# An attention read feeding a squared-ReLU expert: the hidden chunk leaves PSUM once, and the written order is replaced

## The chip, the core and the metric

The kernel runs on one NeuronCore of a Trainium2 chip. TensorE (PE in the rows, its weight loads PEld), VectorE (DVE), ScalarE (ACT), GpSimd (POOL) and SyncE (SP, which issues the DMAs) work side by side and wait for one another on semaphores. The metric is the time of one execution on the device, in microseconds (us).

## The reference, cut to what is computed

```python
# x: (8, 8, 512, 64), state: (8, 8, 32, 64); w_in (512, 2048), w_out (2048, 512) are 8-byte floats
scores = x @ state.T / 8;  a = softmax(scores);   xread = a @ state     # per batch and head
scores2 = state @ x.T / 8; a2 = softmax(scores2); sread = a2 @ x
out = concatenate([xread, sread], axis=2)          # (8, 8, 544, 64)
X = out.transpose(0, 2, 1, 3).reshape(8 * 544, 512)
h = maximum(X @ w_in, 0)
return (h * h) @ w_out                             # (4352, 512)
```

## The kernel before, in words

The tokens are worked in nine blocks: blocks 0 to 7 are the 512 tokens of one batch, block 8 holds the 256 state tokens of all batches. The 2048 hidden columns are cut into 16 chunks of 128. Precision is kept by pairs: a number is held as a high part (type fp32r) and a low part, the rest, and a product is three products, high by high, high by low and low by high.

- `hidden(blk, fc)` makes one chunk of X @ w_in, 128 hidden columns by 512 tokens, in one PSUM bank `ph`: 6 products in blocks 0 to 7 (the weights there are state times w_in, and the softmax values `k_hi`, `k_lo` are the moving side), 8 in block 8. Then it makes the squared ReLU as a pair `g_hi`, `g_lo`. Before the change there are two ways. A chunk in the list `square` has three ScalarE passes, ReLU and square inside PSUM and a cast to `g_hi`; any other has a ReLU to SBUF (`r`), VectorE's product of the ReLU and `r` inside PSUM, and ScalarE's square of `r` as `g_hi`. In both, VectorE takes `g_hi` from the bank for `g_lo`, and only then is the bank free. One chunk (0.1) makes its low part by a product with minus the identity instead (`minus_hi`, list `g_pe`).
- `accumulate(blk, fc)` multiplies the pair by the chunk of w_out, 12 products of 512 columns into four banks `acc` (6 in block 8). In blocks 0 and 1 it comes in two parts, `g_hi` first.
- There are two banks for `ph` (`ps_h`, shared with the dummy products, `later_w2` and part of the joined rows), three buffers for `g_hi` and `g_lo`, and two for the tag `g`, which holds `r` and block 8's `cross`.
- Weights arrive as 8-byte floats and are decoded: a clamp, a ScalarE pass, two integer instructions of VectorE (`decode_wi` for w_in, with a store of the result to `win_f`; `prep_wo` for w_out).
- `warm(i)` is a step of two transposes of the identity whose result nobody reads; there are 12 such steps.
- The order on every engine, SP's DMAs too, is written out: `PLAN` lists steps, and each name runs that step up to its next `yield`. Since `LOOSE_FROM` is never met, every instruction is kept in that order. `SECOND` lists for which keys an operation goes to its second engine (`pick(key, first, second)`), the clamps, low parts, evacuations and softmax steps among them.

An instruction that waits therefore holds all that stands behind it on its engine. All instructions have the line L429 in the profile, that of the helper which issues them, so they are told apart by their tiles.

Of the kernel before, what the change touches and what calls it, by code (L numbers as in the profile page):

```python
# [25 lines left out]
    ident start.0 start.0 load_raw.0 decode_wi.0 load_states.0 load.0.1 decode_wi.0 prep.0.0 load_raw.1  # L26
        warm.0 neg_ident load.0.1 decode_wi.0 load_states.0 warm.5 warm.2 prep.0.1 load_states.0 prep.0.0
        load_wo.1 decode_wi.0 prep.0.0 prep.0.1 decode_wi.0 warm.11 load_wo.0 warm.6 decode_wi.1 prep.0.0
        decode_wi.1 decode_wi.1 warm.8 start.1 prep.0.1 states.0 prep.0.1 load_raw.2 prep_wo.1 states.0
        scores.0 decode_wi.1 start.1 load.1.1 prep_wo.1 prep_wo.1 decode_wi.1 prep_wo.0 direct_w2.0  # L30
        keep_s.0.0 keep_s.0.1 decode_wi.2 transposed_scores.0.1 direct_w2.0 direct_w2.0 warm.10
        transposed_scores.0.0 direct_w2.0 direct_w2.0 prep_wo.1 prep_wo.1 direct_w2.0 load.1.1 load_raw.3
        load_wo.3 direct_w2.0 second_w2.0 softmax.0.1 second_w2.0 softmax.0.1 warm.4 softmax.0.1 second_w2.0
# [4 lines left out]
        warm.3 load_wo.4 decode_wi.3 prep_wo.0 softmax.0.0 prep_wo.1 decode_wi.3 scores.1 keep_s.1.0
        keep_s.1.1 softmax.0.1 decode_wi.3
    hidden.0.0 decode_wi.3 hidden.0.0 hidden.0.0 transposed_scores.1.0 hidden.0.0 load_raw.5 load_wo.6  # L40
        prep_wo.2 prep_wo.2 softmax.1.0 hidden.0.0 prep_wo.0 transposed_scores.1.1 softmax.1.1 softmax.1.1
        decode_wi.3 load_wo.8
    hidden.0.1 softmax.1.0 hidden.0.1 hidden.0.0 accumulate.0.0 softmax.1.1 prep_wo.2 decode_wi.4 hidden.0.1
        hidden.0.1 direct_w2.1 softmax.1.1 direct_w2.1 decode_wi.4 direct_w2.1 prep_wo.3 direct_w2.1
        direct_w2.1 decode_wi.4 direct_w2.1 direct_w2.1 hidden.0.1 prep_wo.2 hidden.0.1 softmax.1.0
        second_w2.1 accumulate.0.0 exp_s.0.1
    hidden.0.2 prep_wo.2 second_w2.1 second_w2.1 hidden.0.2 softmax.1.0 softmax.1.1
    hidden.0.3 prep_wo.3 prep_wo.5 softmax.1.1 hidden.0.2 softmax.1.0 decode_wi.4 accumulate.0.1
        accumulate.0.1 softmax.1.1 decode_wi.4 softmax.1.1 hidden.0.2 hidden.0.3 softmax.1.0 hidden.0.2
        prep_wo.2 second_w2.1 decode_wi.5 second_w2.1 hidden.0.3 exp_s.0.1 load_raw.6 prep_wo.3 second_w2.1  # L50
        prep_wo.3 hidden.0.2 accumulate.0.2 prep_wo.4 softmax.1.0 prep_wo.3 softmax.1.0 decode_wi.6
        decode_wi.5 accumulate.0.2 hidden.0.3 prep_wo.5 prep_wo.4 prep_wo.3
# [6 lines left out]
    hidden.1.2 direct_w2.2 direct_w2.2 decode_wi.10 prep_wo.5 hidden.1.1 hidden.1.2 load_wo.7 accumulate.1.0
        hidden.1.1 accumulate.1.1 load_raw.7 decode_wi.6 hidden.1.2  # L60
    hidden.0.4 exp_s.0.0 hidden.1.2 decode_wi.10 decode_wi.7 decode_wi.7 prep_wo.6 hidden.1.2 second_w2.2
        hidden.1.2 prep_wo.4 decode_wi.7 hidden.0.4 prep_wo.5 exp_s.0.0 second_w2.2 load_raw.11 second_w2.2
        second_w2.2 decode_wi.7 transposes.0 load_states.2 decode_wi.7 accumulate.1.1 second_w2.2 prep_wo.8
        decode_wi.11 hidden.0.4 hidden.0.4 hidden.0.4 prep_wo.4 second_w2.2 prep_wo.6
# [14 lines left out]
    hidden.1.5
    hidden.1.4 prep_wo.10 states.2 hidden.1.5 prep_wo.12 hidden.1.4 hidden.1.4 accumulate.0.6 direct_w2.4  # L80
        decode_wi.12 hidden.1.4 transposes.0 prep_wo.9 decode_wi.12 decode_wi.14 prep_wo.10 hidden.1.4
        hidden.1.5 prep_wo.10 direct_w2.5 hidden.1.4 accumulate.0.6 load_raw.13 accumulate.0.7 hidden.1.5
        hidden.1.5 decode_wi.14 hidden.1.5 prep_wo.12 exp_s.1.1 prep_wo.9 accumulate.0.7 load_w2.0.4
        accumulate.0.7 accumulate.0.7 prep_wo.10 prep_wo.12
    hidden.1.6 load_w2.0.4 accumulate.0.7 prep_wo.10 decode_wi.12 accumulate.0.7
    hidden.1.7 hidden.1.7 hidden.1.6 accumulate.0.7 accumulate.0.7 hidden.1.6 accumulate.0.7 load_n.0.0
        load_n.0.1 decode_wi.14 prep_wo.12 prep_wo.13 prep_wo.12 hidden.1.6 decode_wi.14 hidden.1.6
        decode_wi.13 decode_wi.13 load_w2.0.4 hidden.1.7 accumulate.0.7 accumulate.1.4 prep_wo.11 prep_wo.12
        hidden.1.7 prep_wo.11 accumulate.1.4 load_raw.15 prep_wo.13 accumulate.1.5 exp_s.1.1 decode_wi.14
        hidden.1.6 hidden.1.7 load_w2.0.5 hidden.1.7 accumulate.1.5 decode_wi.13 decode_wi.13 prep_wo.13  # L90
        prep_wo.11 decode_wi.13 prep_wo.11 accumulate.1.6 direct.6+read.0 exp_s.1.0 sread.0 direct_w2.6
        accumulate.1.6 prep_wo.11 accumulate.1.7 accumulate.1.7 direct_w2.6 decode_wi.15 decode_wi.15
        sread.0 load_wo.14 direct_w2.6 decode_wi.15 sread.0 accumulate.1.7 direct_w2.6 load_w2.0.5
    hidden.0.8 prep_wo.13 hidden.0.8 hidden.0.8 accumulate.1.7 load_wf.1.1 decode_wi.15 hidden.0.8
        accumulate.1.7
    hidden.0.9 accumulate.1.7 decode_wi.15 hidden.0.9 direct.7 accumulate.1.7 prep_wo.11 hidden.0.8
        split_states load_w2.0.6 accumulate.1.7 hidden.0.9 sread.0 load_w2.0.5 load_w2.1.6 accumulate.1.7
        exp_s.1.0 hidden.0.8 accumulate.0.8
# [1291 lines left out]
```

## Time and profile before

| | us |
|---|---|
| median of 3 runs (lowest, highest) | 649.44 (648.93, 649.57) |
| the profiled execution, its own time | 649.0 |
| its span, first to last instruction | 647.2 |
| TensorE busy in the span | 634.5 |
| VectorE, ScalarE, GpSimd busy | 365.7, 348.0, 125.9 |

The span is 1.8 us shorter than the profiled execution's time. Busy times overlap one another; a time of an engine counts for the total only where another engine waits for it.

### The profile page before, as it was taken

The page shows a single profiled execution, that of the slowest core. Times are in us where ns is not written, and L with a number is a line of the kernel's source. Part 1 is how long each engine was busy: PE and PEld are TensorE (multiplying, and loading weights), DVE is VectorE, ACT ScalarE, POOL GpSimd, SP SyncE. Part 2 cuts the span into 40 slices and gives each one's busy share as a digit, 9 for nine tenths or more (in the row PEclk, how much of TensorE's full clock was granted, in tenths as well). Part 3 has the DMA queues.
Part 4 walks back from the last instruction along what each step waited for, and adds up shares of the span by engine and source line. Part 5 has one row for each costly group of instructions (what it writes and reads, how often), then busy time and mean ns, then how long its engine had stood idle before and what let it go on. Part 6 is the DMA issues. An engine that isn't in the chain of part 4 may idle for free.

```text
span 647.2 us, 10790 instructions
## 1 busy us (share of the span) xinstructions
PE 634.5 (98%) x4004; PEld 511.6 (79%) x4004; DVE 365.7 (56%) x658; ACT 348.0 (54%) x678; POOL 125.9 (19%) x96
## 2 busy tenths in 40 slices
PE   5899999999999999999999999999999999999997
PEld 4677777888788878778878878788777888888886
DVE  3999896775756467475347545456354554442322
ACT  3888867656655455365444544455444355444433
POOL 1584343413310220022001310021010101001000
PEclk9999999999999999999999999999999999999999
DMA  8877898988866684463665635352779814240103
GB/s 270 314 233 243 291 283 290 265 266 252 228 179 182 196 253 110 99 169 100 147 163 146 149 82 158 86 124 73 239 239 271 216 46 115 67 145 34 32 1 97
DMA packets 151859, 110.87 MB, mean 171 GB/s; under 512 B 93056, under 2 KB 126080, under 8 KB 151808
## 3 DMA queue, kind: packets, MB, share of 16 engines
q1 hardware_dynamic: 151568, 109.93, 58.7%
q8 instruction: 31, 0.51, 0.3%
q10 hardware_dynamic: 240, 0.26, 0.1%
q14 instruction: 20, 0.16, 0.1%
HBM read 71.89 MB, written 38.27 MB: 170 GB/s over the span
## 4 chain that ended last, share of the span: by engine, by line
PE 95%; DVE 3%; DMA 1%; issue 0%; SPq 0%; ACT 0%; DVEq 0%
PE acc L429 58%; PE ph L429 30%; PE w2ps L429 2%; PE w4ps L429 2%; PE pr L429 1%; PE st L429 1%; DMA xn<-in_x_dram 1%; DVE wf L429 1%; DVE s L429 1%; DVE sp L429 1%; DVE m L429 0%; PE px L429 0%; DVE dec L429 0%; SPq L429 0%; PE pw L429 0%
## 5 line engine op out<-in xcount | busy, mean ns | idle before, releaser
L429 PE MATMUL acc<-wo,g_hi 128*128 128x512 f32 x1090 | 322.4, 391 | 0.0
L429 PEld LDWEIGHTS acc<-wo,g_hi 128*128 128x128 f32 x1090 | 202.8, 188 | 47.4 <-issue 3.4
L429 PE MATMUL acc<-wo,g_lo 128*128 128x512 f32 x545 | 196.7, 389 | 0.0
L429 PE MATMUL ph<-k_hi,w 128*128 128x512 f32 x512 | 172.8, 390 | 0.2 <-DVE w L429 0.2
L429 DVE TENSOR_TENSOR g_lo<-ph,g_hi 128x512 fp32r<-128x512 f32 (+1 forms) x143 | 92.9, 655 | 83.4 <-ACT g_hi L429 81.2
L429 PEld LDWEIGHTS acc<-wo,g_lo 128*128 128x128 f32 x545 | 102.1, 188 | 21.9 <-issue 0.4
L429 ACT ACTIVATE ph<-ph 128x512 f32<-128x512 f32 (+1 forms) x150 | 83.1, 554 | 59.3 <-PE ph L429 49.7
L429 PEld LDWEIGHTS ph<-k_hi,w 128*128 128x128 f32 x512 | 96.0, 188 | 21.4 <-DVE w L429 0.6
L429 PE MATMUL ph<-k_lo,w 128*128 128x512 f32 x256 | 99.8, 390 | 0.0
L429 DVE SCALAR_TENSOR_TENSOR ph<-ph,r 128x512 f32<-128x512 f32 (+1 forms) x69 | 46.7, 676 | 87.8 <-ACT r L429 87.8
L429 ACT ACTIVATE r<-ph 128x512 f32<-128x512 f32 (+1 forms) x69 | 40.3, 583 | 86.6 <-PE ph L429 75.0
L429 POOL TENSOR_TENSOR w<-w_f,w 128x512 fp32r<-128x512 f32 x25 | 32.7, 1309 | 178.5 <-ACT w L429 167.4
L429 PEld LDWEIGHTS ph<-k_lo,w 128*128 128x128 f32 x256 | 48.0, 188 | 10.2 <-DVE k_lo L429 0.3
L429 ACT ACTIVATE g_hi<-r 128x512 fp32r<-128x512 f32 (+1 forms) x69 | 42.4, 616 | 23.1 <-PE acc L429 17.4
L429 ACT CAST g_hi<-ph 128x512 fp32r<-128x512 f32 (+1 forms) x75 | 41.7, 556 | 16.2 <-PE acc L429 14.6
L429 ACT CAST w<-w_f 128x512 fp32r<-128x512 f32 x40 | 24.6, 618 | 17.9 <-DMA w_f<-w_d 14.1
L429 POOL TENSOR_SCALAR dec<-wo_raw 128x512 f32<-128x512 f32 x10 | 20.1, 2012 | 15.3 <-DMA wo_raw<-in_moe_w_out_dram 14.9
L429 POOL TENSOR_TENSOR wo<-dec,wo 128x512 fp32r<-128x512 f32 x12 | 16.7, 1393 | 26.7 <-ACT wo L429 20.4
L429 POOL TENSOR_TENSOR sp<-sp,m 128x512 f32<-128x512 f32 x9 | 9.5, 1052 | 63.8 <-DVE m L429 63.8
L429 POOL TENSOR_TENSOR wf<-wf,wf_hi 128x512 fp32r<-128x512 f32 x8 | 10.5, 1318 | 51.8 <-ACT wf_hi L429 51.7
L429 DVE TENSOR_TENSOR ph<-ph,cross 128x256 f32<-128x256 f32 x16 | 6.9, 432 | 23.7 <-ACT cross L429 23.6
L429 POOL TENSOR_TENSOR s<-sf,s 128x512 fp32r<-128x512 f32 x6 | 7.7, 1292 | 64.8 <-ACT s L429 38.1
(115 smaller groups left out, 597.4 us busy)
## 6 DMA issues: line engine op xcount, KB each, us to landing
w_f<-w_d SPq DMA_DIRECT2D x40, 256.0 KB, 3.4
wi_raw<-in_moe_w_in_dram SPq DMA_DIRECT2D x16, 512.0 KB, 4.8
wo_raw<-in_moe_w_out_dram SPq DMA_DIRECT2D x16, 512.0 KB, 5.9
xr<-in_x_dram SPq DMA_DIRECT2D x16, 512.0 KB, 4.8
wf<-win_f SPq DMA_DIRECT2D x16, 512.0 KB, 4.3
w_d<-w4o SPq DMA_DIRECT2D x32, 256.0 KB, 3.0
w<-w2a_d SPq DMA_DIRECT2D x16, 512.0 KB, 4.5
out_dram<-o SPq DMA_DIRECT2D x31, 256.0 KB, 2.9
```

Of the source, the lines that this page charges most:

```text
L429: op = call(*args, **kw)
```

## The change

The squared ReLU is made in one way for all chunks. The bank is read once, by a ReLU to SBUF on ScalarE, or on VectorE for the 55 chunks in the list `relu`. The square of `r` as `g` is made on GpSimd, or on VectorE for the 80 chunks in `square`. ScalarE makes `g_hi` as the square of `r` for all 144. The low part is `g` minus `g_hi`, on VectorE, or on GpSimd for the 68 chunks in `g_lo`. The tag `g` has three buffers, `r` and `g` both take from it, and `neg_ident` moves to the tag `aT`. The product with minus `g_hi` is gone. A dummy step is one matrix product of the identity by itself instead of two transposes. `PLAN` is another order of the same steps throughout, and most lists of `SECOND` are others: on GpSimd stand 4 clamps of w_in and 6 of w_out instead of 6 and 10.

```diff
@@ PLAN, its start
-    ident start.0 start.0 load_raw.0 decode_wi.0 load_states.0 load.0.1 decode_wi.0 prep.0.0 load_raw.1
-        warm.0 neg_ident load.0.1 decode_wi.0 load_states.0 warm.5 warm.2 prep.0.1 load_states.0 prep.0.0
-        load_wo.1 decode_wi.0 prep.0.0 prep.0.1 decode_wi.0 warm.11 load_wo.0 warm.6 decode_wi.1 prep.0.0
-        decode_wi.1 decode_wi.1 warm.8 start.1 prep.0.1 states.0 prep.0.1 load_raw.2 prep_wo.1 states.0
-        scores.0 decode_wi.1 start.1 load.1.1 prep_wo.1 prep_wo.1 decode_wi.1 prep_wo.0 direct_w2.0
...
+    ident start.0 start.0 prep.0.0 load_raw.0 decode_wi.0 decode_wi.0 warm.9 load.0.1 load_states.0 load.0.1
+        load_states.0 prep.0.1 load_states.0 prep.0.0 decode_wi.0 prep.0.1 decode_wi.0 load_raw.1 prep.0.0
+        load_wo.1 prep.0.1 start.1 prep.0.0 states.0 states.0 decode_wi.0 prep.0.1 decode_wi.1 load_raw.2
+        start.1 decode_wi.1 scores.0 keep_s.0.1 decode_wi.2 load.1.1 decode_wi.1 neg_ident warm.0 keep_s.0.0
+        prep_wo.1 prep_wo.1 load_wo.5 transposed_scores.0.1 transposed_scores.0.0 load_wo.0 decode_wi.1
+        load.1.1 load_raw.3 decode_wi.1 direct_w2.0 softmax.0.1 direct_w2.0 prep_wo.1 direct_w2.0
...
@@ SECOND
-    g_pe: 0.1
+    g_lo: 0.1 0.3 0.5 0.6 0.8 0.9 0.10 0.11 0.13 0.14 0.15 1.3 1.4 1.8 1.11 1.15 2.0 2.2 2.3 2.7 2.8 2.10
...
+    relu: 0.6 0.14 0.15 1.5 1.11 1.14 1.15 2.3 2.4 2.8 2.11 3.0 3.1 3.6 3.8 3.10 3.11 3.12 3.13 3.14 3.15
...
@@ warm
-        for k in range(2):
-            nc.tensor.transpose(ps[:, ts(k, P)], ident, ident)
+        nc.tensor.matmul(ps[:, :P], ident, ident, start=True, stop=True)
@@ hidden
-            cross = p2.tile([P, nt], F32, tag="g", name=f"cross{fc}", bufs=2)
+            cross = p2.tile([P, nt], F32, tag="g", name=f"cross{fc}", bufs=3)
...
-        r = None
-        if f"square.{blk}.{fc}" in second:
-            nc.scalar.activation(ph, ph, AF.Relu)
-            yield
-            nc.scalar.activation(ph, ph, AF.Square)
+        r, g = [p2.tile([P, nt], F32, tag="g", name=f"{t}{blk}_{fc}", bufs=3) for t in "rg"]
+        if f"relu.{blk}.{fc}" in second:
+            nc.vector.tensor_scalar_max(r, ph, 0.0)
         else:
-            r = p2.tile([P, nt], F32, tag="g", name=f"r{blk}_{fc}", bufs=2)
             nc.scalar.activation(r, ph, AF.Relu)
-            yield
-            nc.vector.scalar_tensor_tensor(ph, ph, 0.0, r, ALU.max, ALU.mult)
-        yield
-        if r is None:
-            nc.scalar.copy(ghi, ph)
-        else:
-            nc.scalar.activation(ghi, r, AF.Square)
-        yield
-        if blk < NX and fc < HF and f"g_pe.{blk}.{fc}" in second:
-            minus_hi(ph, ghi)
-            yield
-            nc.scalar.copy(glo, ph)
-        else:
-            yield
-            nc.vector.tensor_sub(glo, ph, ghi.bitcast(F32))
+        yield
+        pick(f"square.{blk}.{fc}", nc.gpsimd, nc.vector).tensor_mul(g, r, r)
+        yield
+        nc.scalar.activation(ghi, r, AF.Square)
+        yield
+        pick(f"g_lo.{blk}.{fc}", nc.vector, nc.gpsimd).tensor_sub(glo, g, ghi.bitcast(F32))
@@ negative_ident
-        neg["ident"] = p2.tile([P, P], F32R, tag="stT", name="neg_ident", bufs=1)
+        neg["ident"] = p2.tile([P, P], F32R, tag="aT", name="neg_ident", bufs=1)
```

## Rows read from the trace of the kernel before

**Rows 1.** The page: busy time, share of the span, instructions; the granted clock.

```profile
PE 634.5 (98%) x4004; PEld 511.6 (79%) x4004; DVE 365.7 (56%) x658; ACT 348.0 (54%) x678; POOL 125.9 (19%) x96
...
PEclk9999999999999999999999999999999999999999
```

**Rows 2.** Three stretches: length, each engine's busy time (instructions), granted clock, DMA.

```profile
core 0: us, PE busy (x) PEld busy (x) DVE busy (x) ACT busy (x) POOL busy (x), PEclk, DMA share, GB/s
18.00:37.20 19.20, 17.67 (x150) 12.73 (x150) 18.82 (x35) 16.44 (x35) 12.37 (x8) 1.00 0.84 302
37.20:115.00 77.80, 77.80 (x567) 61.22 (x566) 65.92 (x128) 61.09 (x122) 36.64 (x22) 1.00 0.84 267
115.00:640.00 525.00, 525.00 (x3170) 426.56 (x3169) 272.50 (x481) 261.13 (x506) 73.81 (x59) 1.00 0.54 150
```

**Rows 3.** What TensorE waited for, whole span: us in total, times, longest.

```profile
PE px L429 <- DMA xn<-in_x_dram: 5.8, 2, 3.7
PE w2ps L429 <- ACT w L429: 0.7, 1, 0.7
...
PE ph L429 <- DVE w L429: 0.2, 1, 0.2
```

**Rows 4.** The chain that ended last: start, us, what.

```profile
286.82 2.72 PE acc L429 x12
```

**Rows 5.** The groups of the squared ReLU: xcount | busy us, mean ns | idle before.

```profile
L429 DVE TENSOR_TENSOR g_lo<-ph,g_hi 128x512 fp32r<-128x512 f32 (+1 forms) x143 | 92.9, 655 | 83.4 <-ACT g_hi L429 81.2
...
L429 ACT ACTIVATE ph<-ph 128x512 f32<-128x512 f32 (+1 forms) x150 | 83.1, 554 | 59.3 <-PE ph L429 49.7
...
L429 DVE SCALAR_TENSOR_TENSOR ph<-ph,r 128x512 f32<-128x512 f32 (+1 forms) x69 | 46.7, 676 | 87.8 <-ACT r L429 87.8
L429 ACT ACTIVATE r<-ph 128x512 f32<-128x512 f32 (+1 forms) x69 | 40.3, 583 | 86.6 <-PE ph L429 75.0
...
L429 ACT ACTIVATE g_hi<-r 128x512 fp32r<-128x512 f32 (+1 forms) x69 | 42.4, 616 | 23.1 <-PE acc L429 17.4
L429 ACT CAST g_hi<-ph 128x512 fp32r<-128x512 f32 (+1 forms) x75 | 41.7, 556 | 16.2 <-PE acc L429 14.6
```

**Rows 6.** Two-input instructions on SBUF operands, groups of GpSimd and VectorE.

```profile
L429 POOL TENSOR_TENSOR sp<-sp,s 128x512 f32<-128x512 f32 x11 | 11.8, 1070 | 43.2 <-DVE s L429 39.5 <-DVE r L429 1.4 <-ACT g_hi L429 0.9
...
L429 POOL TENSOR_TENSOR s<-sf,s 128x512 fp32r<-128x512 f32 x6 | 7.7, 1292 | 64.8 <-ACT s L429 38.1 <-PE ph L429 26.7
...
L429 DVE TENSOR_TENSOR s<-sf,s 128x512 fp32r<-128x512 f32 x10 | 6.9, 687 | 1.5 <-ACT s L429 1.4
```

**Rows 7.** The timeline, 7 to 19 us: start, us, instruction [idle before].

```profile
7.20 0.43 DVE L429 TENSOR_SCALAR wf<-wi_raw 128x512 f32<-128x512 f32 x1 [7.20 <-DMA wi_raw<-in_moe_w_in_dram]
...
9.91 1.49 PE L429 MATMUL pw<-ident 128*128 128x128 f32 x6
...
11.19 0.68 PE L429 MATMUL px<-ident,xn 128*128 128x128 f32 x4
...
12.34 0.59 ACT L429 COPY sD<-pd 128x512 f32<-128x512 f32 x1 [1.39 <-PE pd L429]
...
12.98 1.10 PE L429 MATMUL st<-xT,sD 64*32 64x256 f32 x32 [0.67 <-DVE dec L429]
...
13.87 1.07 PE L429 MATMUL w2ps<-wf,sD 64*32 64x256 f32 x32
...
18.06 0.88 PE L429 MATMUL pw<-ident 128*128 128x128 f32 x6
```

**Rows 8.** The timeline, 24 to 36 us.

```profile
24.88 1.29 DVE L429 TENSOR_TENSOR k_lo<-pa,k_hi 128x512 fp32r<-128x512 f32 x2
...
25.30 0.51 PE L429 MATMUL ph<-k_hi,w 128*128 128x512 f32 x1
...
32.11 0.50 PE L429 MATMUL ph<-g_hi,neg_ident 128*128 128x512 f32 x1
...
34.85 0.73 PE L429 MATMUL ph<-k_hi,w 128*128 128x512 f32 x2 [0.18 <-DVE w L429]
```

**Rows 9.** The timeline of VectorE and GpSimd, 116 to 121 us.

```profile
116.75 1.48 POOL L429 TENSOR_TENSOR wf<-wf,wf_hi 128x512 fp32r<-128x512 f32 x1 [4.75 <-ACT wf_hi L429]
116.99 1.78 DVE L429 TENSOR_TENSOR wo<-dec,wo 128x512 fp32r<-128x512 f32 x1
```

More of the change, by code (lines that the diff above doesn't have):

```diff
@@ L40 @@
[L40 to L52, printed above, removed]
@@ L59 @@
[L59 to L64, printed above, removed]
@@ L79 @@
[L79 to L98, printed above, removed]
-    hidden.0.10 load_wf.1.0 hidden.0.9 prep_wo.13 split_states exp_s.1.0 hidden.0.9 hidden.0.9
-        accumulate.0.8 hidden.0.10 load_w2.0.6 start.2 hidden.0.10 hidden.0.10 load_w2.0.6 direct_w2.7
@@ new lines @@
+    hidden.2.12 load_w2.3.0 later_w2.7 hidden.2.10 hidden.2.10 hidden.2.12 later_w2.7 hidden.2.11
+        hidden.2.10 prep.3.1 accumulate.2.8 w2.1+scores.3 transposes.2 last_w2.1 accumulate.2.9 hidden.2.11
+        hidden.2.11 last_w2.1 later_w2.7 transposed_scores.3.0
+    hidden.2.13 accumulate.2.10 hidden.2.12 softmax.3.0 hidden.2.11 hidden.2.13 last_w2.1 softmax.3.0
+        transposed_scores.3.1 load_w2.2.7 exp_s.3.0 hidden.2.12 accumulate.2.11 load_w2.2.7 load_n.2.0
+        load_w2.3.0 softmax.3.1 exp_s.3.1 prep.4.0 softmax.3.0 last_w2.1 start.5 softmax.3.0 start.5
+        load_w2.2.7 softmax.3.1 exp_s.3.0 hidden.2.13
@@ new lines @@
+    hidden.2.14 start.5 softmax.3.0 hidden.2.12 softmax.3.1 softmax.3.0 accumulate.2.12 hidden.2.13
+        hidden.2.14 load_w2.3.0 hidden.2.13 softmax.3.1 softmax.3.1 softmax.3.0
+    hidden.2.15 exp_s.3.0 softmax.3.0 load_w2.3.2 hidden.2.14 hidden.2.15 last_w2.1 softmax.3.1 load_w2.3.2
+        softmax.3.1 hidden.2.14 read.2 softmax.3.1 last_w2.1 hidden.2.14 accumulate.2.13 exp_s.3.1 start.5
+        hidden.2.15
+    hidden.3.0 hidden.2.15
+    hidden.3.3 accumulate.2.14 hidden.3.3 hidden.2.15 load_w2.3.6 hidden.3.3 hidden.3.3
@@ new lines @@
+    hidden.3.4 load_w2.3.6 transposes.3 accumulate.3.1 hidden.3.4 prep.4.1 hidden.3.2 hidden.3.4
+        w2.0+scores.4 last_w2.0 transposed_scores.4.1 load.5.1 last_w2.0 softmax.4.1 load_w2.3.6 hidden.3.4
+        accumulate.3.2 hidden.3.4 hidden.3.5 last_w2.0 hidden.3.5 transposes.3
+    hidden.3.6 hidden.3.5 load_wf.2.2 start.6 softmax.4.1 transposed_scores.4.0 accumulate.3.3 hidden.3.6
+        transposes.3 prep.5.0 accumulate.3.4
+    hidden.3.8 softmax.4.0 last_w2.0 softmax.4.0 last_w2.0 transposes.3 start.6 load_w2.3.5 transposes.3
+        exp_s.4.1
```

616 lines of the change are left out of this document (308 added, 308 removed), and 3 rows, old and new, of the table SECOND.

## Prediction

> **What bounds the kernel now.** I began with the page. TensorE is busy 634.5 of 647.2 us, at a granted clock that reads 9 or more tenths in all 40 slices; the other engines stand at 56, 54 and 19% [rows 1]. A busy share says nothing of waits, so I read next what TensorE waited for: 8.7 us over the span, of which the first transfers of x are 5.8, and the last entry is 0.2 us for a weight tile [rows 3]. Asked for 37 to 640 us alone, the same view has no entry. The stretches say the same: TensorE is busy for all of 77.8 us from 37.2 to 115 and all of 525 us from 115 to 640, at 1.00 [rows 2], the higher of the clock's two levels, 2.4 GHz. The reader should see that for 600 us the time is a number of products and nothing else. Their pace is in the chain: 12 products of 512 columns take 2.72 us, 0.227 each [rows 4], so a hidden chunk is 6 x 0.227 = 1.36 us and an accumulate 2.72.
>
> The products stay the same but for one, so the change can gain only where TensorE is not yet full: before 37 us. There the limit is another. From 18 to 37.2 us VectorE is busy 18.82 of 19.20 us and ScalarE 16.44 [rows 2]; the first hidden chunk starts at 25.30 us, while VectorE makes the two low parts that it needs, 24.88 to 26.17 [rows 8].
>
> **The squared ReLU.** ScalarE loses 75 ReLUs and 75 squares at 554 ns (83.1 us), 75 casts (41.7), 69 ReLUs (40.3) and 69 squares (42.4), 207.5 in all [rows 5]. It gets 144 squares at 616 ns, 88.7, and 144 - 55 = 89 ReLUs at 583, 51.9: some 67 us less. VectorE loses 92.9 + 46.7 = 139.6 us [rows 5] and gets 55 ReLUs, for which no row stands; the nearest is a low part out of PSUM, 655 ns, 36 us. It also gets 80 squares and 76 low parts from SBUF at 687 ns [rows 6], 107: in all 143, about what it had. GpSimd gets 64 squares, nearest 1070 ns, and 68 low parts, nearest 1292 [rows 6], 68 + 88 = 156 us on top of 125.9. No engine is full by this, and all of it lies beside TensorE's products: worth 0 on the path.
>
> That cover is the distance between a chunk and its accumulate. Counting products in the two orders at 0.227 us, the median distance is 9.0 us before and 13.1 after. The new way at its slowest is ReLU 0.58 + square 1.07 + low part 1.29 = 2.94 us against 0.58 + 0.68 + 0.66 or so before (ScalarE's square runs beside). So the cover is larger on the whole. It is thinner in two respects, both counted in the orders. First, 38 of 144 low parts stand less than 1.5 us of products ahead of the accumulate that reads them, 25 before, and 19 of the 38 are GpSimd's, none before. Second, the bank is freed by the ReLU and no longer by the low part, and the new order uses this: in 19 places the next user of a chunk's bank stands less than 1.5 us behind that chunk, in 2 before. A ReLU takes 0.58 once its engine is free; if the instruction ahead of it (0.55 to 0.69) has just begun, the product waits some 0.3. All 17 new places missed by 0.3 are 5 us, none missed is 0. I take one in five, 1 us less what the longer distances save where nothing waits today, that is nothing: +0.5 to +1, and put +0.7. With the third buffer of `g`, a ReLU still needs the buffer that the low part two chunks back frees; where that low part is GpSimd's, the ReLU waits with all that stands behind it on its engine. I count this among the same places.
>
> **The dropped product.** Chunk 0.1's product with minus `g_hi` starts at 32.11 and the next at 32.45 [rows 8]: -0.34. That product is one that must be made on the saturated engine; bounds -0.23 (its bare pace) and -0.75 (with TensorE's wait of 0.4 us for `g_hi` in front of its weights).
>
> **The start.** I followed both written orders by hand, engine by engine, with durations from the rows. (1) Of the dummy steps, six transposes stand from 9.91 to 11.19 in front of the last transposes of block 0 [rows 7]. After, none does, and the second half of group 1 of x is issued ahead of `wi_raw1`. I take the scores' start to move from 12.98 to about 12.3, not by the whole 1.28, since `sD`, 0.59 at 12.34 [rows 7], still follows the transposes, and these run at the slow early pace: six small products took 1.49 us at 9.91 and 0.88 at 18.06 [rows 7]. (2) `wi_raw1` now comes behind two transfers of x and three of the state, and the last instruction of its decode behind `keep_s` and a clamp on VectorE. So `w2ps` of the first chunk pair, 13.87 before [rows 7], comes at about 15.3, +1.4. (3) ScalarE then has the same 25 instructions to the last evacuation of block 1's x, with the copies of `w2ps` among them, and ends about 0.7 later. (4) VectorE has 34 instructions to the second low part instead of 30, 43 instead of 38 to the low part of chunk 0.0, and 64 instead of 59 to the last low part of block 1. The four clamps come from GpSimd at 0.4 us each, the two maxima of `exp_s` are drawn ahead, and the low part of w_out's chunk 1 comes from GpSimd. That is +1.5 to +2.5 us of an engine that has 0.4 us to spare in 19 [rows 2]. (5) Against this the squares of the first chunks are on GpSimd, the order puts the weights of chunk pair 1 so that the wait which ends at 34.85 [rows 8], 0.34 us, goes, and three hidden chunks stand in a row where the softmax of block 1 is late. Block 1's first chunk, though, comes 1.1 us of products earlier, and needs the low part that VectorE makes 2.5 us of work later: the margin of about 3 us goes to about 0.
>
> By these steps the first chunk ends 0.2 to 1 us later, and the accumulate of chunk 0.1 ends where it did, within my error. I put the start at 0, with -2 (step 1 whole and the wait of step 5) and +2.5 (all of step 4) as bounds. What is late then is block 1's first chunk, and behind it on TensorE everything.
>
> The other dummy steps fill idle time: 24 products before, 12 after, in places where TensorE waits for VectorE or ScalarE. Their cost and gain are 0 while it waits; with that cover gone six took 0.88 [rows 7], so 1.8 for twelve, within the bounds above. The granted clock shows 1.00 in every slice there, so from the rows a denser dummy buys nothing. The Trainium skill ("TensorE: Matmul & The Clock Gate", Part 4) says that transposes do not bring the clock up as products do. By that rule the early pace would improve with the new dummies; but here four transposes took 0.68 at 11.19 after nothing but transposes [rows 7], so the trace does not bear it out, and only one of the new products stands ahead of the first scores: by the rule at most some 0.6 us, by the row 0.
>
> **Sum.** -0.34 (product) + 0 (start) + 0.7 (tight places) = +0.36 on the profiled 649.0, which is its span of 647.2 and 1.8 around it: 649.4. The median of the runs is 649.44, 0.44 above the profiled one, and would give 649.8; I take the middle, 649.6. The end is the same in both orders (block 8's last half accumulate, ScalarE's copy, a store).
>
> **Rivals.** *Faster:* the start gains and nothing is missed later. The scores' 0.7 reach the first chunk because VectorE and ScalarE find their operands without the waits that I put in, and the 0.34, the 0.34 of step 5 and the 0.4 in front of the dropped product go whole: 649.4 - 1.8 = 647.6. For it: larger distances, ScalarE 67 us lighter. Against: ScalarE and VectorE are full from 18 us on.
>
> *Slower:* VectorE and GpSimd block one another. At 116.75 GpSimd starts a low part of 1.48 us, and VectorE's, begun at 116.99, takes 1.78 [rows 9] where its like takes 0.69 alone [rows 6]: it waited for GpSimd. Low parts read from PSUM show no such thing: mean 655 over 143 [rows 5]. The change takes VectorE's squares and low parts to SBUF and doubles GpSimd's work. With GpSimd at 282 of 647 us, 44%, and half of 1.1 to 1.3 us waited in a hit, each of the 156 instructions loses about 0.26, 41 us of VectorE, and the first 115 us, where it is busy 66 of 78 even after 37.2 [rows 2], have about 35 of them, 9 us. It decides from the point where VectorE has nothing left, that is where these 9 and the 2.5 of step 4 pass its 12 free us: half of such an excess lands on TensorE, 2 us, for 651.4. The Trainium skill ("SBUF — State Buffer", Who interferes with whom) states this as a rule, a VectorE instruction with two SBUF inputs contends with a GpSimd one that reads SBUF, and speaks so against the change; by it, too, low parts left in PSUM would cost nothing.
>
> *Slower at the start alone:* all of step 4 holds and TensorE stalls for block 1: 649.4 + 2.1 = 651.5.
>
> **Numbers.** What a measurement of this kernel tells from no change is 0.2%, 1.3 us. Chances: the forecast 0.41, faster 0.32, VectorE with GpSimd 0.17, the start 0.10. So faster 0.32, same 0.41, slower 0.27. The forecast's own range is 648.2 to 650.7. The faster case reaches to 647 (its 1.8 and the rest of step 1), the slower ones to 652.3 (one of them with half of the tight places' 5 us on top); beyond these I leave 0.2.
>
> **What would show it.** In the profile after: no entry for TensorE's waits beyond 45 us, or entries for `ph` on `r` (tight places) and for `acc` on `g_lo` by GpSimd (cover gone); `st` at 12.3 and `w2ps` at 15.3; the first `ph` between 25.5 and 26.5; ScalarE near 280 us, GpSimd near 280. VectorE's SBUF squares well above 687 ns mean would show the blocking, and TensorE's share from 37 to 115 us below all of it that it matters. The prediction is wrong if the start shifts by over 1.3 us, or if TensorE's time from 115 to 640 us grows.

## The result, and the profile after

The changed kernel takes 656.78 us, the median of four runs (655.27 to 661.17), against 649.51 for the kernel before beside it: ratio 1.0119, 95% interval 1.0094 to 1.0143. Forecast were 649.6 us and at most 652.3. The profiled execution took 656.33 us with a span of 654.5, so 1.8 us lie around the span as before.

The page of the changed kernel (that of the kernel before is in [rows 1]): busy times and granted clock, the shares of the chain that ended last, by engine and by line, and VectorE's part of the squared ReLU.

```profile
PE 637.0 (97%) x4003; PEld 510.9 (78%) x4003; DVE 406.1 (62%) x673; ACT 276.7 (42%) x542; POOL 275.7 (42%) x217
...
PEclk9999999999999999999999999999999999999999
...
PE 83%; DVE 10%; issue 2%; DMA 2%; POOL 1%; ACT 1%; SPq 0%; DVEq 0%; POOLq 0%
PE acc L414 50%; PE ph L414 26%; DVE wf L414 3%; DVE dec L414 2%; PE w4ps L414 2%; PE w2ps L414 2%; PE pr L414 1%; PE st L414 1%; DVE g_lo L414 1%; DMA xn<-in_x_dram 1%; DVE wo L414 1%; DVE s L414 1%; PE px L414 1%; DVE w L414 1%; DMA w_f<-w_d 0%
...
L414 DVE TENSOR_TENSOR g<-r 128x512 f32<-128x512 f32 (+1 forms) x80 | 63.4, 793 | 45.3 <-ACT r L414 27.8
L414 DVE TENSOR_TENSOR g_lo<-g,g_hi 128x512 fp32r<-128x512 f32 (+1 forms) x76 | 60.6, 799 | 38.7 <-ACT g_hi L414 33.3
...
L414 DVE TENSOR_SCALAR r<-ph 128x512 f32<-128x512 f32 (+1 forms) x55 | 36.4, 665 | 50.6 <-PE ph L414 43.8
```

The chain of the kernel before, by engine:

```profile
PE 95%; DVE 3%; DMA 1%; issue 0%; SPq 0%; ACT 0%; DVEq 0%
```

ScalarE has lost 71 us and GpSimd has won 150, about as worked out ahead; VectorE was to stay where it was and has won 40. About half of the 40 is the squared ReLU (139.6 us before, 160.4 now). VectorE's share of the chain has gone from 3 to 10%, and its largest entries there are `wf` and `dec`, which are the decode of weights and no part of the squared ReLU.

The stretches of the changed kernel (PE, PEld, DVE, ACT, POOL busy, granted clock, DMA share, GB/s; before: [rows 2]):

```profile
18.00:37.20 19.20, 18.10 (x149) 12.98 (x148) 18.79 (x35) 15.29 (x33) 13.46 (x10) 1.00 0.98 349
37.20:115.00 77.80, 74.32 (x545) 56.49 (x545) 75.14 (x125) 47.67 (x95) 43.76 (x30) 1.00 0.72 228
115.00:640.00 525.00, 524.26 (x3163) 425.29 (x3162) 296.76 (x486) 203.65 (x395) 215.92 (x171) 1.00 0.55 152
```

TensorE was busy in all of the second stretch before and now stands for 3.5 us of it, while VectorE went from 65.92 to 75.14 of 77.80 us. TensorE's waits in the changed kernel (total, times, longest) name the late ones; in the kernel before the same view has no entry from 37 to 640 us:

```profile
...
PE ph L414 <- DVE k_lo L414: 1.0, 1, 1.0
PE pa L414 <- POOL sp L414: 0.8, 2, 0.6
PE w2ps L414 <- DVE wf L414: 0.8, 1, 0.8
PE ph L414 <- DVE w2o L414: 0.8, 1, 0.8
...
PE acc L414 <- DVE wo L414: 0.6, 1, 0.6
...
```

The first hidden chunk starts at 25.82 us (25.30 before), and from there to the last product's start it is 624.4 us (617.7 before). So in this execution 0.5 us of the loss lie at the start and 6.6 behind it. Read from the starts of the products, eight gaps of more than 0.2 us behind the first 37 make 5.5 of it, five of them (4.2 us) ended by VectorE. A second profile of the same kernel (e15 below) has six of the eight again, ended by the same tiles.

What lengthened VectorE is seen by groups of like instructions from 37.2 to 115 us (busy us, mean ns). The kernel before:

```profile
L429 DVE SCALAR_TENSOR_TENSOR wf<-wi_raw,wf 128x512 uint32<-128x512 uint32 x12 | 9.6, 797 | 0.1
L429 DVE SCALAR_TENSOR_TENSOR dec<-wo_raw,dec 128x512 uint32<-128x512 uint32 x11 | 9.0, 820 | 0.1
...
L429 DVE TENSOR_SCALAR wf<-wi_raw 128x512 f32<-128x512 f32 x7 | 2.9, 414 | 0.7 <-DMA wi_raw<-in_moe_w_in_dram 0.6
...
L429 DVE TENSOR_SCALAR dec<-wo_raw 128x512 f32<-128x512 f32 x4 | 1.6, 409 | 0.9 <-POOL w L429 0.9
...
L429 DVE TENSOR_TENSOR wo<-dec,wo 128x512 fp32r<-128x512 f32 x2 | 1.4, 678 | 0.0
```

and the changed kernel:

```profile
L414 DVE SCALAR_TENSOR_TENSOR wf<-wi_raw,wf 128x512 uint32<-128x512 uint32 x12 | 11.6, 970 | 0.1
L414 DVE SCALAR_TENSOR_TENSOR dec<-wo_raw,dec 128x512 uint32<-128x512 uint32 x10 | 9.8, 977 | 0.1
...
L414 DVE TENSOR_TENSOR wo<-dec,wo 128x512 fp32r<-128x512 f32 x6 | 6.6, 1105 | 0.0
L414 DVE TENSOR_TENSOR g_lo<-g,g_hi 128x512 fp32r<-128x512 f32 x9 | 6.5, 736 | 0.0
L414 DVE TENSOR_SCALAR dec<-wo_raw 128x512 f32<-128x512 f32 x7 | 6.4, 918 | 1.2 <-POOL wo L414 1.2
L414 DVE TENSOR_SCALAR wf<-wi_raw 128x512 f32<-128x512 f32 x9 | 5.5, 607 | 0.0
...
L414 DVE TENSOR_TENSOR g<-r 128x512 f32<-128x512 f32 x5 | 3.4, 681 | 0.3 <-ACT r L414 0.3
```

The same decode instructions got longer; the squares and low parts of the new way, which the prediction watched, hardly did in this stretch. With one further kind (`wf<-wf`, 501 to 581 ns) the lengthening is 12 x 0.17 + 10 x 0.16 + 7 x 0.51 + 6 x 0.43 + 12 x 0.08 + 9 x 0.19 = 12.5 us.

The stretch also holds more of them. The new side lists take clamps and low parts of the weights from GpSimd, so VectorE has 7 clamps of w_out instead of 4, 9 of w_in instead of 7 and 6 low parts of w_out instead of 2: at the old durations some 4.8 us. Its part of the squared ReLU fell there from 14.4 to 11.3 us, and what comes later than before falls out of the stretch. So the 9.2 us by which VectorE's busy time rose are not lengthening alone.

One case, in time (start, duration), of VectorE, GpSimd and TensorE:

```profile
63.28 1.71 DVE L414 SCALAR_TENSOR_TENSOR wf<-wi_raw,wf 128x512 uint32<-128x512 uint32 x1
63.16 1.29 POOL L414 TENSOR_TENSOR g_lo<-g,g_hi 128x512 fp32r<-128x512 f32 x1 [0.19 <-ACT g_hi L414]
65.14 0.63 PE L414 MATMUL w2ps<-wf,sD 64*32 64x256 f32 x11 [0.81 <-DVE wf L414]
```

GpSimd has begun a low part 0.12 us ahead; VectorE's decode instruction, 0.68 us alone, ends half a microsecond after GpSimd's; and TensorE, which needs the decoded weights, stands for 0.81.

### The profile page after: what moved, and what is told of

It reads as the page before. It is cut to its first block, busy times and chain, and to the rows that moved or that the text cites. A ratio compares the mean times of both kernels' runs of the same rounds, so it can differ in the third digit from the quotient of the medians.

```text
span 654.5 us, 10890 instructions
## 1 busy us (share of the span) xinstructions
PE 637.0 (97%) x4003; PEld 510.9 (78%) x4003; DVE 406.1 (62%) x673; ACT 276.7 (42%) x542; POOL 275.7 (42%) x217
## 4 chain that ended last, share of the span: by engine, by line
PE 83%; DVE 10%; issue 2%; DMA 2%; POOL 1%; ACT 1%; SPq 0%; DVEq 0%; POOLq 0%
PE acc L414 50%; PE ph L414 26%; DVE wf L414 3%; DVE dec L414 2%; PE w4ps L414 2%; PE w2ps L414 2%; PE pr L414 1%; PE st L414 1%; DVE g_lo L414 1%; DMA xn<-in_x_dram 1%; DVE wo L414 1%; DVE s L414 1%; PE px L414 1%; DVE w L414 1%; DMA w_f<-w_d 0%
## 5 line engine op out<-in xcount | busy, mean ns | idle before, releaser
L414 POOL TENSOR_TENSOR g_lo<-g,g_hi 128x512 fp32r<-128x512 f32 (+1 forms) x68 | 91.6, 1349 | 132.1 <-ACT g_hi L414 103.5
L414 ACT ACTIVATE g_hi<-r 128x512 fp32r<-128x512 f32 (+1 forms) x144 | 87.3, 608 | 139.9 <-PE acc L414 102.2
L414 POOL TENSOR_TENSOR g<-r 128x512 f32<-128x512 f32 (+1 forms) x64 | 72.7, 1135 | 151.4 <-ACT g_hi L414 25.5
L414 DVE TENSOR_TENSOR g<-r 128x512 f32<-128x512 f32 (+1 forms) x80 | 63.4, 793 | 45.3 <-ACT r L414 27.8
L414 DVE TENSOR_TENSOR g_lo<-g,g_hi 128x512 fp32r<-128x512 f32 (+1 forms) x76 | 60.6, 799 | 38.7 <-ACT g_hi L414 33.3
L414 ACT ACTIVATE r<-ph 128x512 f32<-128x512 f32 (+1 forms) x89 | 50.3, 568 | 74.1 <-PE ph L414 58.4
L414 DVE TENSOR_SCALAR r<-ph 128x512 f32<-128x512 f32 (+1 forms) x55 | 36.4, 665 | 50.6 <-PE ph L414 43.8
L414 PEld LDWEIGHTS ph<-k_lo,w 128*128 128x128 f32 x256 | 48.1, 188 | 11.4 <-DVE k_lo L414 1.8
L414 ACT CAST w<-w_f 128x512 fp32r<-128x512 f32 x40 | 24.6, 618 | 36.6 <-PE ph L414 14.9
L414 POOL TENSOR_TENSOR s<-sf,s 128x512 fp32r<-128x512 f32 x9 | 11.8, 1313 | 11.4 <-ACT s L414 9.7
L414 ACT CAST w2h<-w2ps 128x512 fp32r<-128x512 f32 x16 | 9.3, 581 | 16.6 <-PE w2ps L414 13.2
L414 DVE COPY o<-acc 128x512 f32<-128x512 f32 (+1 forms) x13 | 8.7, 668 | 12.1 <-PE acc L414 9.3
```

The source lines that it names most:

```text
L414: op = call(*args, **kw)
```

## The experiments

Theory A: GpSimd's new instructions and VectorE's SBUF instructions hold one another up while weights are decoded, and VectorE's lateness reaches TensorE. Theory B: the new order and the other sides are late whatever the squared ReLU. Theory C came later: the dummies and TensorE's clock at the start. The table has each run's median, the ratio to the kernel before in the same runs with its interval, and from the profile: the start of the first hidden chunk, the time from there to the last product's start, and TensorE's and VectorE's busy time from 37.2 to 115 us (77.80).

| run | us | ratio (95%) | first chunk | rest | PE | DVE |
|---|---|---|---|---|---|---|
| before | 649.5 | | 25.3 | 617.7 | 77.80 | 65.92 |
| changed | 656.78 | 1.0119 (1.0094-1.0143) | 25.8 | 624.4 | 74.32 | 75.14 |
| e15, changed again | 657.24 | 1.0105 (1.0083-1.0127) | 28.3 | 624.8 | 75.06 | 75.07 |
| e5 before + GpSimd products | 655.48 | 1.0089 (1.0074-1.0104) | 26.0 | 623.6 | 73.62 | 70.10 |
| e6 before + GpSimd fills | 652.64 | 1.0045 (1.0030-1.0060) | 25.9 | 622.0 | 75.23 | 68.05 |
| e13 the same products, late | 649.72 | 0.9997 (0.9987-1.0007) | 24.6 | 617.7 | 77.80 | 65.71 |
| e12 before + VectorE work | 654.36 | 1.0070 (1.0051-1.0089) | 25.3 | 623.3 | 75.44 | 72.70 |
| e4 early ReLU^2 off GpSimd | 659.44 | 1.0144 (1.0127-1.0161) | 28.2 | 625.1 | 75.95 | 72.35 |
| e7 early squares off GpSimd | 653.42 | 1.0049 (1.0030-1.0067) | 26.4 | 620.1 | 77.23 | 70.32 |
| e10 and off VectorE | 652.12 | 1.0038 (1.0019-1.0056) | 28.6 | 618.7 | 77.44 | 70.21 |
| e11 and low parts left out | 650.75 | 1.0012 (0.9997-1.0028) | 26.1 | 616.7 | 77.80 | 62.64 |
| e1 new ReLU^2, old order | 678.45 | 1.0443 (1.0427-1.0458) | 24.9 | 648.0 | 69.40 | 67.57 |
| e3 new order, old sides | 674.77 | 1.0399 (1.0369-1.0430) | 30.0 | 638.7 | 67.63 | 63.97 |
| e9 old dummies | 655.76 | 1.0090 (1.0059-1.0120) | 25.9 | 622.1 | 75.45 | 74.78 |
| e14 three dummies moved ahead | 657.77 | 1.0122 (1.0104-1.0140) | 27.9 | 624.6 | 74.35 | 74.80 |
| e19 the same, transposes | 656.67 | 1.0108 (1.0089-1.0127) | 28.3 | 622.4 | 75.07 | 75.55 |
| e16 e14's move in e10 | 653.65 | 1.0061 (1.0046-1.0076) | 27.4 | 620.2 | 77.22 | 67.71 |
| e20 three dummies more | 657.28 | 1.0112 (1.0072-1.0151) | 25.8 | 626.9 | 75.08 | 74.14 |
| e21 the same in e10 | 656.38 | 1.0093 (1.0072-1.0113) | 26.8 | 623.5 | 75.24 | 68.77 |
| e18 before, dummies moved back | 650.59 | 1.0019 (1.0008-1.0029) | 27.3 | 619.2 | 77.66 | 66.22 |

**GpSimd work that nobody reads.** The kernel before, in its order, with one product added wherever the change gives GpSimd a square or a low part:

```diff
+        if f"load_sq.{blk}.{fc}" in second:      # the 64 squares; likewise load_lo, the 68 low parts
+            nc.gpsimd.tensor_mul(junk, junk, junk)   # 128x448, SBUF
```

> The kernel before with GpSimd instructions added that nobody reads: one product of 448 columns in SBUF for each of the 64 squares and 68 low parts that the change gives to GpSimd, at their places in the old order. Theory A: VectorE's SBUF instructions lengthen by some 10 us in all from 37 to 115 us, and the kernel gets slower, 650.5 to 655 us. Theory B: 649 to 650 us, since nothing waits for the added instructions.

It cost 5.9 us. VectorE's decode groups in that run, from 37.2 to 115 us, beside a low part read from PSUM:

```profile
L427 DVE SCALAR_TENSOR_TENSOR wf<-wi_raw,wf 128x512 uint32<-128x512 uint32 x12 | 12.3, 1029 | 0.1
L427 DVE TENSOR_TENSOR g_lo<-ph,g_hi 128x512 fp32r<-128x512 f32 x16 | 10.6, 678 | 0.8 <-ACT g_hi L427 0.7
L427 DVE SCALAR_TENSOR_TENSOR dec<-wo_raw,dec 128x512 uint32<-128x512 uint32 x11 | 10.3, 940 | 0.1
```

They lengthen as in the changed kernel; the PSUM low part stays at 678 ns (685 before). Nothing else of the change was made, so a load of this kind on GpSimd is by itself enough for most of what the change lost. It is not the changed kernel's load to the microsecond: GpSimd is busy for 56.67 us from 37.2 to 115 us here and for 43.76 there. All of this run's stalls of over 0.2 us behind the first 37 lie before 103 us, though only 21 of the 132 products stand before 115. Two of them, 1.0 and 0.5 us near 41 us, are GpSimd's own low part of w_out and a softmax product that came late behind the added work. The next run asks how much of it is that.

```diff
-            nc.gpsimd.tensor_mul(junk, junk, junk)
+            [nc.gpsimd.memset(junk, 1.0) for _ in range(2)]
```

> As the kernel before with GpSimd's unread work, but each added product is two fills of 448 columns (0.47 us each, as the one fill of that run took), which write SBUF and read nothing; GpSimd's own instructions stand behind them as they stood behind the products. Theory A1 (VectorE and GpSimd block one another where both read SBUF): the unlengthened 0.68 us for VectorE's two-input decode instructions from 37 to 115 us, and 649.5 to 652 us. Theory A2 (GpSimd's own clamps and low parts come late behind the added work, whatever it reads): about 655 us again.

It cost 2.8 us (4.2 behind the first chunk in its profile), above A1's range and half of what the products cost. Counted over this trace, 12 of VectorE's two-input SBUF instructions met fills alone: 650 to 694 ns, none longer than alone. But 11 one-input ones that met fills alone took 606 ns on average, against 421 for the 16 that met nothing, and GpSimd's clamps and low parts, moved against VectorE's work, hit the two-input ones elsewhere. VectorE's two instructions on raw weights in that run (min/median/max ns, from 37.2 to 115 us)

```profile
L427 DVE SCALAR_TENSOR_TENSOR wf<-wi_raw,wf x12: 628/693/1747, 38.2 to 108.2; 128x512 uint32<-128x512 uint32 x12
L427 DVE TENSOR_SCALAR wf<-wi_raw x7: 414/650/769, 54.3 to 95.6; 128x512 f32<-128x512 f32 x7
```

show both. So neither A1 nor A2 is alone: GpSimd's products and subtractions, which read, hold up VectorE's two-input instructions, its fills, which only write, hold up the short one-input ones alone, and the late queue costs the same two stalls near 41 us. The Trainium skill ("SBUF — State Buffer", Who interferes with whom) says that an instruction with two SBUF inputs contends with a GpSimd one that reads, not with one that only writes. The trace agrees, with the numbers above. The same section says that VectorE's two-port modes contend with GpSimd; that the one-input instructions run in such a mode is not seen in these traces, only that fills lengthen them.

**The same load where VectorE has room.**

```diff
+    # load_sq, load_lo: blocks 2 to 8 alone
```

> The kernel before with GpSimd's unread products for blocks 2 to 8 alone (44 and 52 of the 64 and 68). VectorE is busy 272 of 525 us there. Theory A: its instructions lengthen as much per hit, but nothing waits: 649 to 650.5 us. If contention costs TensorE wherever it is: about 654.

No difference, though VectorE's instructions lengthen there too: its low parts of the weights `wf<-wf,wf_hi` go from a median of 682 to 972 ns (mean 994 to 1070), and its busy time from 115 to 640 us rises by 4.0 us, about as much as in e5 from 37.2 to 115 (4.2).

**VectorE's time by itself.**

```diff
+        if f"load_sq.{blk}.{fc}" in second:      # blocks 0 and 1, 16 chunks; the kernel before
+            [nc.vector.transpose(junk[:, 0], junk[:, 1]) for _ in range(2)]
```

> The kernel before with work added on VectorE that nobody reads: two transposes of 224 columns (an estimate of 0.3 us each from the 0.70 of 512 columns) behind the ReLU of the 16 early chunks whose square the change gives to GpSimd, some 10 us in all before 115 us. GpSimd gets nothing. If what costs TensorE its time is VectorE's lengthened time and nothing else of GpSimd: 652 to 656 us, a third to two thirds of the 10. If VectorE has slack to hide 10 us (12 free before): 649.5 to 650.5.

The 32 transposes took 0.35 to 0.41 us each, 13 us, 8.9 of them from 37 to 115 us. TensorE lost 5.6 us behind the first chunk, although VectorE stayed idle for 5.1 us of that stretch. The 12 us that VectorE has free there in the kernel before were no reserve. The added transposes stand in the chain of the squared ReLU, ahead of the low part that frees the bank, and this run does not tell what the same time would cost at other places.

**GpSimd's early work taken away from the changed kernel,** in three steps (chunks 0 to 11 of blocks 0 and 1):

```diff
# e7: the 16 squares of GpSimd; e10: all early squares, and all early ReLUs
+        if blk < NX and fc < 12 and f"square.{blk}.{fc}" not in second:
+            nc.scalar.activation(g, r, AF.Square)
# e11, on top of e10: GpSimd's 12 early low parts, the subtraction left out
+            nc.scalar.copy(glo, g)
# e4, on top of e7: those 12 low parts on VectorE
+            nc.vector.tensor_sub(glo, g, ghi.bitcast(F32))
```

> The changed kernel with the 16 squares that GpSimd makes of chunks 0 to 11 of blocks 0 and 1 on ScalarE (0.57 each, 9 us of its 30 free from 37 to 115 us); the low parts stay where the change puts them, so VectorE gets nothing. Theory A: of VectorE's 9 us of longer instructions a half goes, and 652.5 to 655 us. Theory B (order and sides): 656 to 658 us.

> As the run before with all squares and ReLUs of chunks 0 to 11 of blocks 0 and 1 on ScalarE, VectorE's 8 squares and 2 ReLUs too: VectorE loses some 5 us of work from 37 to 115 us on top. Theory A in the form that VectorE's time is what sets the stalls: 650.5 to 653 us. If ScalarE becomes late in its place, waits for r or g_hi by ScalarE show, and 653 to 657 us. Theory B: 656 us or more.

> As the run with all early squares and ReLUs on ScalarE, and the 12 low parts that GpSimd makes of chunks 0 to 11 of blocks 0 and 1 replaced by a ScalarE copy of the square: the subtraction of these 12 is left out, so that neither GpSimd nor VectorE has them. GpSimd then has no work of the squared ReLU before block 0's chunk 12. Theory A: VectorE's busy time from 37 to 115 us falls from 70.2 to about 66, and 649.5 to 651.5 us. Theory B (something of the order or the other sides is late besides): 652 us or more, with the stalls at the same places.

> The changed kernel with the 16 squares and 12 low parts that GpSimd makes of chunks 0 to 11 of blocks 0 and 1 given to ScalarE and VectorE; order and other sides stay new. Theory A: VectorE's decode instructions fall back to about 800 ns, the stalls from 40 to 115 us mostly go, 650 to 652.5 us, though VectorE gets 12 more low parts of 0.69. Theory B: 655 to 657.5 us, as the changed kernel or slower.

Sixteen squares fewer on GpSimd give back 3.4 of the changed kernel's 656.8 us, and the two-input decode stands at 684 ns again (e7, first line below); with VectorE's squares and ReLUs gone too, 4.7; without any early work of the new way on GpSimd, 6.0, and the stretch shows a full TensorE (e11, second line):

```profile
L414 DVE SCALAR_TENSOR_TENSOR wf<-wi_raw,wf 128x512 uint32<-128x512 uint32 x12 | 8.2, 684 | 0.1
...
37.20:115.00 77.80, 77.80 (x568) 61.05 (x567) 62.64 (x124) 63.09 (x127) 18.33 (x11) 1.00 0.80 254
```

The first step stands out of the noise; the intervals of e7 and e10, and of e10 and e11, overlap. So nothing of the new order's late stalls remains in e11, with the new order and the new sides in place, and theory B falls for the time behind the start. (The profiled execution of e11 took 648.98 us, all ten 648.98 to 653.02.) Since e11 takes early work from VectorE as well, it is e7 that shows GpSimd's share. What the decode work that the side lists put on VectorE costs was not measured by itself. The fourth run was expected at 650 to 652.5 and is the slowest of them: 12 low parts of 0.69 us put on VectorE cost more than GpSimd's hold-ups had, though 1.9 us of the 6.0 between e7 and e4 is a later first chunk, of which more below. TensorE stands for 2.1 us up to 152.8, waiting for an evacuation on VectorE, and then its granted clock falls:

```profile
150.00:152.00 2.00, 0.91 (x5) 0.41 (x3) 2.00 (x2) 1.69 (x4) 1.34 (x1) 1.00 0.05 8
152.00:154.00 2.00, 1.16 (x3) 0.80 (x4) 2.00 (x5) 0.00 (x0) 0.00 (x0) 0.85 0.18 68
154.00:156.00 2.00, 2.00 (x8) 1.22 (x8) 1.79 (x3) 0.00 (x0) 0.00 (x0) 0.50 0.98 252
```

**Order and sides the other way round.**

```diff
# e1: the kernel before with the new ReLU^2, its lists relu, square, g_lo, and three buffers of g
# e3: the changed kernel with all other lists as before
```

> The new squared ReLU (lists relu, square, g_lo, three buffers of g) in the order and with the other sides of the kernel before. Theory A (GpSimd's new instructions and VectorE's SBUF instructions lengthen one another while weights are decoded): VectorE's decode instructions from 37 to 115 us last longer than in the kernel before (its 797 and 820 ns go to about 970), TensorE stalls there, 652 to 657 us. Theory B (the new order and the other sides are late whatever the chain): 649 to 650 us, no stall beyond 45 us.

> The changed kernel with all side lists but those of the squared ReLU as they were before (clamps, low parts of weights, evacuations, softmax): GpSimd gets 2 clamps of w_in and 4 of w_out and 6 low parts of w_out's chunks back. Theory A: VectorE has fewer instructions but GpSimd more that lengthen them, 654 to 659 us. Theory B, if the sides are what is late: 650 to 653 us; if the order is: about 656.

Both are far slower than either theory said. In the first TensorE waits for low parts by GpSimd (4.8 us) and for evacuations by VectorE (4.6): the old order leaves fewer products between a chunk and its accumulate, so a GpSimd low part is not hidden. In the second `ph` waits 5.0 us for ReLUs. Parts of the change made for one another can't be priced by putting one of them into the other frame; these two runs only say that.

**The dummies.** First the old dummies in the changed kernel, then the changed kernel once more:

> The changed kernel with two transposes as a dummy step again in place of one product. Theory A and theory B: no difference, 656 to 657.5 us, the granted clock 1.00 in the same slices. If the dummies matter: over 1 us either way, and the first chunk's start away from 25.8 us.

> The changed kernel once more, as the measure for the runs that start from it: 655 to 658 us by every theory.

The dummies' kind is not told apart (653.8 to 657.5 us). But the second profile of the same kernel has its first chunk 2.5 us later. Its scores (32 products) take 1.96 us there, in the profile after 1.10, and the eight transposes behind them are slow as well. The first line is of the profile after, the others of the second one:

```profile
11.71 1.10 PE L414 MATMUL st<-xT,sD 64*32 64x256 f32 x32 [0.68 <-ACT sD L414]
...
12.82 1.96 PE L414 MATMUL st<-xT,sD 64*32 64x256 f32 x32 [0.68 <-ACT sD L414]
...
15.66 1.60 PE L414 MATMUL pst<-ident,e 128*128 128x128 f32 x8
```

That is TensorE's lower clock, told by the pace: the 128-column steps before it rises take 0.213 us, as they do in e14 below where the column reads 0.50, and then 0.109. In the old order, six dummy transposes between the transposes of x [rows 7] make TensorE's work unbroken from 8.15 to 12.3 us, the steps go from 0.213 to 0.109 at 11.4, and the scores took 1.10 in every profile with the dummies there. Theory C: without them the clock rises before the scores only when x arrives early (7.6 to 8.01 us in four profiles, scores in 1.10) and not when it arrives at 8.03 to 8.5 (e3, e4, e10, e15, scores in 1.96). The work ahead of the scores is unbroken in e15 too, from 8.47 to 12.15 us, so what decides is not read from these rows.

```diff
# e14: warm.5 warm.11 warm.7 moved ahead of scores.0; e19: the same, one transpose each; e16: e14 and e10
# e20, e21: three dummy products more there, in the changed kernel and in e10
# e18: the kernel before, warm.11 warm.6 warm.8 moved behind scores.0
```

> The changed kernel with three of its dummy products moved ahead of the first scores, into TensorE's wait of 0.67 us for sD. Theory C (without dummies there TensorE's clock rises before the scores in some executions and only after them in others): the scores' 32 products take 1.10 us, the first chunk starts at 25.5 to 26.5 us, median 655 to 656 us, and no time over 658. If the late clock has another cause: scores of 1.96 us in part of the profiles and times up to 660 as before.

> As the first of these runs with one transpose per dummy step in place of the product. If transposes keep TensorE's clock as products do: as that run, 655 to 656 us, scores in 1.10 us. If not: scores in 1.96 us in part of the profiles and times to 660.

> The same move in the run with all early squares and ReLUs on ScalarE. Theories A and C add up: 649.5 to 651.5 us with a spread under 2 us. If C is wrong: 650.4 to 655.6 as that run had without the move.

> The kernel before with the three dummy steps that stand ahead of block 0's last transposes (six transposes, 1.28 us) moved behind the scores. Theory C: the scores come 1.28 us earlier, but take 1.96 us in part of the executions; times then spread, 648 to 652.5 us, median 649 to 651. If the dummies' place is nothing to the clock: 648.5 to 650 us and 1.10 us.

> The changed kernel with three dummy products more, ahead of the first scores, the twelve others at their places. Theory C: scores in 1.10 us, no 1.96; the following w2ps products at their fast pace; first chunk 25.5 to 26.5 us; median 655 to 656, nothing over 658. If the late start is not the clock's: first chunk at 28 in part of the profiles, times to 660.

> The same three dummies in the run with all early squares and ReLUs on ScalarE: 650 to 651.5 us with a spread under 2 us by theories A and C together, still not below the kernel before; 650.4 to 655.6 if C is wrong.

In the old order the theory holds: e18 takes 650.59 us (1.0019, 1.0008 to 1.0029; up to 652.8), its scores 1.96 with x at 8.27, where e6, with the dummies in place, has 1.10 with x at 8.45. What was taken away there are transposes, and in the kernel before the pace doubles at 11.4 us after nothing but transposes, so transposes do bring the clock up here. The Trainium skill ("TensorE: Matmul & The Clock Gate", Part 4) says that they do not count as products do; these runs speak against it. In the new order the move does not pay. e14 has its scores in 1.09 with x at 8.34, but takes 657.77 us: behind the places that the dummies left, the granted clock falls, from 1.00 at 17 to 19 us to 0.72 and 0.50, and the first chunk comes at 27.9.

```profile
17.00:19.00 2.00, 1.25 (x33) 0.50 (x17) 2.00 (x5) 0.56 (x2) 0.47 (x1) 1.00 1.02 407
19.00:21.00 2.00, 1.49 (x6) 1.22 (x7) 1.93 (x5) 2.00 (x6) 0.00 (x0) 0.72 1.05 386
21.00:23.00 2.00, 1.96 (x9) 1.67 (x9) 1.93 (x6) 1.46 (x5) 1.16 (x2) 0.50 1.04 414
```

It falls in e19 too (0.56 at 21 to 23 us) but not in e16, which has the same move, so that the missing dummies let it fall is likely and not shown. e19 took 656.67 us (scores 1.48), e16 653.65, e20 657.28 (653.4 to 662.9) and e21 656.38; only e18 came out as its theory had it. In e20 the first chunk came at 25.8, but x came at 7.14 us there, by theory C early enough for that without the added dummies. The loss moved: `ph` waited 1.3 us for a copy of ScalarE at 206 us. In e21 `ph` waited 2.7 us until 56.9: VectorE stood 0.95 us for raw weights, its clamp then took 1.18 beside a low part of w_out on GpSimd, its own low part came late, and ScalarE's ReLU waited for the buffer of `g` which that frees. So the clock at the start is a real part of the scatter, and not what sets the median. Why e21 is slower than e10, which differs by three products, stays open.

## Why the prediction was wrong

- *What bounds the kernel*: right. The loss is time in which TensorE waits: 0.5 us at the start and 5.5 in eight gaps make 6.0 of the 7.3 us by which the span grew; the rest is in smaller gaps that were not followed up.
- *The squared ReLU, "no engine is full by this, and all of it lies beside TensorE's products: worth 0 on the path"*: this step failed. It summed the engines' times as if they added no time to one another, and it took what lies beside TensorE as free. The runs showed 5.9 us for GpSimd's load alone (e5), of which 2.8 remain with fills that read nothing (e6), and 3.4 us back when 16 early squares leave GpSimd (e7). VectorE's squared ReLU was summed at 687 ns for each new SBUF instruction, 143 us, and took 160.4: squares 793 ns, low parts 799 on the mean. The other half of VectorE's 40 us is no part of that sum: 16 more instructions of other kinds, six clamps and six low parts of w_out among them, which the side lists moved from GpSimd, and the longer decode.
- ScalarE (276.7 us, about 280 forecast) came as summed. GpSimd (275.7, 282) did so by luck: its new instructions were longer than their rows (1135 and 1349 ns against 1070 and 1292), and the side lists took some 19 us of clamps and low parts from it, which the sum left in.
- *The rival in which VectorE and GpSimd block one another* had the mechanism. That its totals fit, 41 us of VectorE (measured 40) and 9 us before 115 us (9.2), is luck: it laid all of it on the 156 new instructions, and these lengthened by about 17 us in all, by under 1 from 37.2 to 115 us, where the decode did. It also let the loss count only beyond 12 free microseconds, half of the excess, 2 us. The runs showed no such threshold: 13 us of VectorE time alone cost 4.8 (e12), though the 8.9 of them in this stretch are fewer than the 12 free. At that price, 0.4, the rival's 9 + 2.5 us would have given 654, still below what was measured.
- *Tight places, +0.7*: the size came out, at other places. A ReLU late for `ph` cost 0.24 us at 55 us, a low part late for its accumulate 0.35 at 100 us; that one was VectorE's, and none of the 19 GpSimd low parts was late. e11 has neither wait, with the same order.
- *Dropped product, -0.34*: nothing in the runs contradicts it, and it is too small to be seen here.
- *The start, 0*: +0.5 in the first profile and +3.0 in the second (e15), where the scores ran at the lower clock; the bound was +2.5. In the first, `st` came at 11.71 (12.3 forecast), `w2ps` at 14.70 (15.3), the first chunk at 25.82 (25.5 to 26.5). Block 1's first chunk, put at a margin of about 0, waited 1.0 us for `k_lo` at 45.4, which was behind a clamp of 1.26 and a decode of 1.52 us that ran beside GpSimd's squares: the margin was lost by contention.
- *The dummies, 0*: not so. Moving three steps of them from ahead of the scores costs the old order 1.2 us (0.5 to 1.9 by the interval). The prediction read the clock column's 1.00 as the higher level there, and the pace tells otherwise.

No run made from the changed kernel beats the one before; with the early work left out it comes to 650.75, and the interval of that ratio takes in 1.

## What to carry to other kernels

An engine's busy time can grow through instructions that nobody edited: when work moves to GpSimd, list VectorE's SBUF instructions that run beside it, and price those too. Free time of the second-busiest engine is no reserve while the bottleneck reads its results in a fixed order; here 13 us put on it, 8.9 of them in a stretch where it had 11.9 free, cost 4.8. That price is no constant: 12 low parts moved to VectorE, some 8 us, cost 6.0 (e7 to e4, with a later start in it), and ten instructions taken from it, some 7 us, gave back 1.3 (e7 to e10, within the intervals). And work moved off the path is free only where the engines have room: here 132 unread products cost 5.9 us, and the 96 of them in blocks 2 to 8 nothing.

## What was not expected of the hardware

- GpSimd's plain fills, which read nothing, lengthen VectorE's one-input SBUF instructions (0.42 us alone, 0.61 beside fills, in e6) and not its two-input ones (0.68 either way).
- A TensorE wait of 2.1 us in the middle of the kernel (e4) was followed by a granted clock of 0.85 and 0.50 in the stretches of 2 us from 152 and 154. Such a stall costs more than its length.
- Until the first rise of the clock the windows' clock column reads 1.00 although the level is the lower one: the scores' 32 products in 1.96 us instead of 1.10 tell it (e15), as do 128-column steps of 0.213 us instead of 0.109.
